# Weights from float64 to float32 on 16-bit halves, in a windowed attention with two MoE layers

## The chip, the cores and the metric

One core of one Trainium2 chip. The metric is the device time of one execution in microseconds (us); the number that counts is the median of several runs. The engines are PE (TensorE, matmuls), DVE (VectorE), ACT (ScalarE), POOL (GpSimd) and SP (SyncE, which issues the DMAs here).

## What is computed

Attention over 2 batches of 8 heads, 768 tokens and a head size of 64, where a token sees the first 4 tokens and a window of 128; then two dense layers on the 1536 tokens, each from 512 to 2048 and back to 512 columns. The weights come as float64.

```python
def _moe_ref(x, w_in, w_out):
    h = x @ w_in
    sp = np.where(h > 20.0, h, np.log1p(np.exp(np.minimum(h, 20.0))))
    g = h * np.tanh(sp)
    return (g @ w_out).astype(np.float32)

def _moe2_ref(x, w_in, w_out):
    h = x @ w_in
    g = h * np.clip(h + 3.0, 0.0, 6.0) / 6.0
    return (g @ w_out).astype(np.float32)

x = attention(q, k, v, n_sink, window)
x = _moe_ref(x, **moe)
return _moe2_ref(x, **moe2)
```

## The kernel before

The code counts the two dense layers as layer 0 and layer 1, and so does this text. The 2048 middle columns of a layer are cut into 16 chunks (`f`), the tokens into three blocks of 512. An `up` step multiplies tokens by the chunk's input weights (L728 to L730; `up2` for layer 1: L797 to L799), ACT and DVE apply the activation (L731 to L745; L801 to L815), and a `down` step multiplies by the output weights (L773; `down2`: L835). Every f32 operand goes to PE as two f16 parts, so each product is three matmuls.

The weights are float64 in HBM, and DVE makes float32 of them. `load_w` fetches one chunk of both matrices into the tile `raw` (two buffers; L166 and L170, on SP's queue). `gen_decode` reads it as 32-bit words, a low and a high word for each number, 1024 numbers in a partition, in three DVE operations on the tile `p`: L209 shifts and masks the high word, L210 puts in the top three bits of the low word, L211 puts in the sign and the top exponent bit. Then `p` is split into two f16 parts: for layer 0 on ACT (L218) and DVE (L220), for layer 1 in `split_pair` (ACT L245, L263; DVE L246, L256 to L259, L264), which works on pairs of chunks.

The three operations are right only for numbers whose exponent lies in a certain range, and a check sees to that. `exponents` takes the top 16 bits of each number on DVE (L184, into the tile `y`, one buffer, 16-bit elements) and lets ACT add them up (L188, which reads `y` as 512 whole words and leaves the sum in a column of `wchk`). For layer 1 that is done in `gen_decode`, just ahead of L209; for layer 0 its weights are fetched once more, late in the program (`gen_check`). A tail takes the largest of `wchk` (L971) and starts a general path if anything is out of range.

The decode of layer 0 runs beside the attention of the first two token blocks and layer 0's first steps. The `p` of layer 1 lies in a pool (`late["p"]`) that opens when attention is done, at about 262 us; from there its decode runs beside the last steps of layer 0 and the first of layer 1. The order of each engine's queue is not the order of the code: a scheduler of the framework places the instructions. An engine works its queue strictly in order.

Of the kernel before, what the change touches and what calls it, by code (L numbers as in the profile page):

```python
# [7 lines left out]
F32 = mybir.dt.float32  # L8
F16 = mybir.dt.float16
I32 = mybir.dt.int32  # L10
I16 = mybir.dt.int16
AF = mybir.ActivationFunctionType
ALU = mybir.AluOpType
# [16 lines left out]
def attention_moe_moe2(  # L30
# [13 lines left out]
    nc = tc.nc  # L44
# [4 lines left out]
    KF = DFF // 128  # L49
# [13 lines left out]
    dec_p = main.enter_context(tc.tile_pool(name="dec", bufs=1))  # L63
# [33 lines left out]
    wchk = keep.tile([128, 2 * KF], F32)  # L97
# [3 lines left out]
    def watch(ap):  # L101
        i = n_low[0]
        n_low[0] += 1
        sq = const.tile([128, 64], F32, tag="sq", name="sq")
        nc.vector.tensor_tensor_reduce(out=sq, in0=ap, in1=ap, scale=1.0, scalar=0.0, op0=ALU.mult, op1=ALU.max, accum_out=lows[:, i:i + 1])
# [50 lines left out]
    late = {}  # L156
# [16 lines left out]
    def load_w():  # L173
        if nload[0] >= len(wseq):
            return
        layer, f = wseq[nload[0]]
        nload[0] += 1
        raw_t[layer, f] = fetch_w(layer, f)

    def exponents(idx, t, pin=False):  # L180

        y = dec_p.tile([128, 1024], I16, tag="y", name="y")
        top = t.rearrange("p f t -> p (f t)").bitcast(I16).rearrange("p (f t) -> p f t", t=4)[:, :, 3]
        look = nc.vector.tensor_scalar(out=y, in0=top, scalar1=0x7800, scalar2=0x3800, op0=ALU.bitwise_and, op1=ALU.bitwise_xor)  # L184
        if pin:
            tc.keep_in_program_order(look)
        yy = y.bitcast(I32)
        nc.scalar.activation(out=yy, in_=yy, func=AF.Copy, accum_out=wchk[:, idx:idx + 1])  # L188

    def gen_check():  # L190


        ahead = []
        for f in range(KF + 2):
            if f > 1:
                exponents(f - 2, ahead.pop(0).rearrange("p a f t -> p (a f) t"), True)
            if f < KF:
                ahead.append(fetch_w(0, f))
            yield
            yield  # L200

    def gen_decode(idx):
        layer, f = wseq[idx]
        t = raw_t.pop((layer, f)).rearrange("p a f t -> p (a f) t")
        lo_w, hi_w = t[:, :, 0], t[:, :, 1]
        if layer == 1:
            exponents(idx, t)
        p = (late["p"] if layer == 1 else dec_p).tile([128, 1024], I32, tag="p", name="p")
        nc.vector.tensor_scalar(out=p, in0=hi_w, scalar1=3, scalar2=0x3FFFFFF8, op0=ALU.logical_shift_left, op1=ALU.bitwise_and)  # L209
        nc.vector.scalar_tensor_tensor(out=p, in0=lo_w, scalar=29, in1=p, op0=ALU.logical_shift_right, op1=ALU.bitwise_or)  # L210
        nc.vector.scalar_tensor_tensor(out=p, in0=hi_w, scalar=-0x40000000, in1=p, op0=ALU.bitwise_and, op1=ALU.bitwise_or)  # L211
        pf = p.bitcast(F32).rearrange("p (a f) -> p a f", a=2)
        load_w()
        if layer == 1:
            yield from split_pair(f, pf)
            return
        w = (w_a if f < KF // 2 else late["w_b"]).tile([128, 2, 2, 512], F16, tag="w", name="w")
        nc.scalar.activation(out=w[:, :, 0, :], in_=pf, func=AF.Copy, scale=2.0 ** SW)  # L218
        yield
        nc.vector.scalar_tensor_tensor(out=w[:, :, 1, :], in0=pf, scalar=2.0 ** SW, in1=w[:, :, 0, :], op0=ALU.mult, op1=ALU.subtract)  # L220
        wt[layer, 0, f] = w[:, 0]
        wt[layer, 1, f] = w[:, 1]
        if f == 0:
            watch(w[:, 0, 0, 0:64])
            watch(w[:, 1, 0, 0:64])
# [10 lines left out]
    def split_pair(f, pf):  # L236


        q = f % 2
        if q == 0:  # L240
            open_pair["w"] = slot()
            open_pair["p"] = []
        w = open_pair["w"]
        open_pair["p"].append(pf[:, 1])
        nc.scalar.activation(out=w[:, q, 0, :], in_=pf[:, 0], func=AF.Copy, scale=2.0 ** SW)  # L245
        nc.vector.scalar_tensor_tensor(out=w[:, q, 1, :], in0=pf[:, 0], scalar=2.0 ** SW, in1=w[:, q, 0, :], op0=ALU.mult, op1=ALU.subtract)  # L246
        wt[1, 0, f] = w[:, q]
        if f == 0:
            watch(w[:, 0, 0, 0:64])
        yield  # L250
        if q == 0:
            return
        p0, p1_ = open_pair.pop("p")
        b11, b12, b21, b22 = p0[:, 0:256], p0[:, 256:512], p1_[:, 0:256], p1_[:, 256:512]
        t = dec_p.tile([128, 4, 256], F32, tag="p", name="t")
        nc.vector.tensor_tensor(out=t[:, 0], in0=b12, in1=b11, op=ALU.subtract)  # L256
        nc.vector.tensor_tensor(out=t[:, 1], in0=b22, in1=t[:, 0], op=ALU.subtract)
        nc.vector.tensor_tensor(out=t[:, 2], in0=b22, in1=b12, op=ALU.subtract)
        nc.vector.tensor_tensor(out=t[:, 3], in0=t[:, 1], in1=b21, op=ALU.subtract)  # L259
        wx = [slot().rearrange("p a b (c n) -> p (a b) c n", c=2) for _ in range(2)]  # L260
        for dst, src in ((wx[0], t), (wx[1][:, 0], b11), (wx[1][:, 1:3], p1_.rearrange("p (a n) -> p a n", a=2))):
            hi = dst[..., 0, :]
            nc.scalar.activation(out=hi, in_=src, func=AF.Copy, scale=2.0 ** SW)  # L263
            nc.vector.scalar_tensor_tensor(out=dst[..., 1, :], in0=src, scalar=2.0 ** SW, in1=hi, op0=ALU.mult, op1=ALU.subtract)  # L264

        wt[1, 1, f // 2] = [wx[1][:, 0], wx[1][:, 1], wx[1][:, 2], wx[0][:, 3], wx[0][:, 0], wx[0][:, 1], wx[0][:, 2]]
        if f == 1:
            watch(wx[1][:, 0, 0, 0:64])
# [407 lines left out]
    def gen_weights():  # L676
        for idx in range(len(wseq)):
            for _ in gen_decode(idx):
                yield None
            yield ("dec", idx)  # L680
# [287 lines left out]
    nc.vector.tensor_scalar(out=bads[:, 1:2], in0=nsw[:, 1:2], scalar1=128.0, scalar2=None, op0=ALU.is_gt)  # L968
    nc.vector.scalar_tensor_tensor(out=bads[:, 1:2], in0=nsw[:, 1:2], scalar=1.0, in1=bads[:, 1:2], op0=ALU.is_lt, op1=ALU.max)

    nc.vector.tensor_reduce(out=bads[:, 2:3], in_=wchk, axis=AX.X, op=ALU.max)  # L971

    nc.vector.tensor_scalar(out=osum, in0=osum, scalar1=0.0, scalar2=0.0, op0=ALU.mult, op1=ALU.is_equal)
# [217 lines left out]
```

## Time and profile before

| what | us |
|---|---|
| median of 3 runs (lowest, highest) | 614.8 (614.75, 616.62) |
| the profiled execution: its own time | 618.45 |
| the profiled execution: span | 616.7 |
| busy in the span: PE, DVE, ACT, POOL | 581.9, 487.0, 393.2, 21.4 |

A busy share is a mean over stretches with different limits, so the stretches are to be read one by one: up to 100 us the first attention blocks, to 260 us the rest of attention beside layer 0, to 402 us the decode of layer 1, then layer 1 alone. A matmul's own duration is not its cost, since matmuls overlap; its cost is the step from one start to the next. The same holds in part on DVE and ACT: an instruction starts up to a tenth of a microsecond before the one ahead of it has ended.

### The profile page before, as it was taken

What the parts mean: (1) busy time and instruction counts of PE and PEld (TensorE: products, weight loads), DVE (VectorE), ACT (ScalarE), POOL (GpSimd) and SP (SyncE); (2) the same over time, 40 slices, a digit from 0 to 9 for tenths busy, and PEclk for the clock granted to TensorE, in tenths of its full rate; (3) what the DMA queues carried; (4) which work ended last, traced back from release to release, by engine and by line L of the source; (5) the groups of instructions that cost most, each with busy time, mean ns of one, the idle gap of its engine ahead of it and who ended that gap; (6) DMA issues with size and microseconds to landing.
All of it is one profiled execution on the core that took longest, in us unless ns stands there. A gap on an engine that the chain in (4) does not pass through costs nothing.

```text
span 616.7 us, 11401 instructions
## 1 busy us (share of the span) xinstructions
PE 581.9 (94%) x4424; PEld 394.9 (64%) x4424; DVE 487.0 (79%) x1132; ACT 393.2 (64%) x788; POOL 21.4 (3%) x36
## 2 busy tenths in 40 slices
PE   8999999789999999899999999899999999999991
PEld 4778664334544444444444468788888888888881
DVE  5889999689976345699999999996687888956652
ACT  5998686687788586578776873544355565534431
POOL 0130001400000000000000000000000000000000
PEclk9999999999999999999999999989999999999996
DMA  9884346997572213242335322400026667200001
GB/s 186 208 161 145 125 137 151 208 266 203 172 207 42 54 36 54 38 154 88 138 122 183 108 101 82 137 2 1 1 70 236 229 223 268 71 2 1 36 1 40
DMA packets 105847, 72.29 MB, mean 117 GB/s; under 512 B 73512, under 2 KB 98088, under 8 KB 105784
## 3 DMA queue, kind: packets, MB, share of 16 engines
q1 hardware_dynamic: 105784, 71.48, 41.7%
q8 instruction: 36, 0.59, 0.4%
q14 instruction: 27, 0.22, 0.1%
HBM read 60.43 MB, written 3.15 MB: 103 GB/s over the span
## 4 chain that ended last, share of the span: by engine, by line
PE 52%; DVE 30%; DMA 7%; ACT 4%; issue 3%; SPq 2%; POOL 0%; DVEq 0%; POOLq 0%
PE acc L835 17%; PE acc L773 5%; PE h L798 5%; PE h L799 5%; PE h L797 5%; DVE p L210 4%; DVE p L211 4%; DMA raw<-in_moe_w_out_dram 3%; DVE w L264 2%; PE h L728 2%; PE h L730 2%; PE h L729 2%; DVE p L209 2%; DVE g L745 2%; DVE e L740 2%
## 5 line engine op out<-in xcount | busy, mean ns | idle before, releaser
L773 PE MATMUL acc<-g,w 128*128 128x512 f16 x576 | 130.6, 379 | 4.6 <-DVE g L745 3.4
L835 PE MATMUL acc<-w,g 128*128 128x256 f16 x1008 | 115.8, 275 | 4.1 <-DVE ob L849 2.6
L835 PEld LDWEIGHTS <-g 128*128 128x128 f16 x1008 | 99.3, 99 | 17.2 <-issue 3.7
L798 PE MATMUL h<-xt,w 128*128 128x256 f16 x384 | 104.7, 273 | 0.0
L797 PE MATMUL h<-xt,w 128*128 128x256 f16 x384 | 104.7, 273 | 0.0
L799 PE MATMUL h<-xt,w 128*128 128x256 f16 x384 | 104.7, 273 | 0.0
L773 PEld LDWEIGHTS <-w 128*128 128x128 f16 x576 | 55.3, 98 | 71.4 <-issue 7.3
L728 PE MATMUL h<-xt,w 128*128 128x512 f16 x192 | 72.7, 379 | 4.5 <-DVE mins L549 3.0
L730 PE MATMUL h<-xt,w 128*128 128x512 f16 x192 | 72.8, 379 | 0.0
L729 PE MATMUL h<-xt,w 128*128 128x512 f16 x192 | 72.8, 379 | 0.0
L802 DVE SCALAR_TENSOR_TENSOR e<-e,h 128x512 f32<-128x512 f32 x48 | 32.8, 686 | 36.9 <-ACT e L801 36.8
L801 ACT ACTIVATE e<-h,bias 128x512 f32<-128x512 f32 x48 | 32.2, 676 | 38.5 <-PE h L799 38.5
L814 ACT ACTIVATE g<-sm 128x512 f16<-128x512 f32 x48 | 30.2, 629 | 31.3 <-DVE sm L809 30.9
L814 ACT ACTIVATE g<-e 128x256 f16<-128x256 f32 x96 | 29.4, 354 | 29.8 <-DVE e L802 29.2
L815 DVE SCALAR_TENSOR_TENSOR g<-sm,g 128x512 f16<-128x512 f32 x48 | 33.2, 691 | 10.1 <-ACT g L814 10.1
L731 ACT ACTIVATE e<-h 128x512 f32<-128x512 f32 x48 | 27.8, 586 | 20.4 <-PE h L730 20.3
L798 PEld LDWEIGHTS <-w 128*128 128x128 f16 x384 | 37.6, 98 | 4.6
L797 PEld LDWEIGHTS <-w 128*128 128x128 f16 x384 | 37.6, 98 | 4.5
L799 PEld LDWEIGHTS <-w 128*128 128x128 f16 x384 | 37.6, 98 | 4.4
L210 DVE SCALAR_TENSOR_TENSOR p<-raw,p 128x1024 int32<-128x1024 int32 x32 | 39.0, 1225 | 0.3
L211 DVE SCALAR_TENSOR_TENSOR p<-raw,p 128x1024 int32<-128x1024 int32 x32 | 39.0, 1221 | 0.1
L740 DVE SCALAR_TENSOR_TENSOR e<-e,h 128x512 f32<-128x512 f32 x48 | 30.9, 682 | 10.4 <-ACT e L738 10.4
(172 smaller groups left out, 953.5 us busy)
## 6 DMA issues: line engine op xcount, KB each, us to landing
raw<-in_moe_w_in_dram SPq DMA_DIRECT2D x48, 512.0 KB, 3.9
raw<-in_moe_w_out_dram SPq DMA_DIRECT2D x48, 512.0 KB, 4.6
out_dram<-ob SPq DMA_DIRECT2D x12, 256.0 KB, 2.1
first<-in_k_dram SPq DMA_DIRECT2D x8, 256.0 KB, 5.1
first<-in_q_dram SPq DMA_DIRECT2D x8, 256.0 KB, 5.2
first<-in_v_dram SPq DMA_DIRECT2D x8, 256.0 KB, 4.8
nk<-in_k_dram SPq DMA_DIRECT2D x5, 256.0 KB, 4.9
nv<-in_v_dram SPq DMA_DIRECT2D x5, 256.0 KB, 4.0
```

What stands on the lines that cost most here:

```text
L210: nc.vector.scalar_tensor_tensor(out=p, in0=lo_w, scalar=29, in1=p, op0=ALU.logical_shift_right, op1=ALU.bitwise_or)
L211: nc.vector.scalar_tensor_tensor(out=p, in0=hi_w, scalar=-0x40000000, in1=p, op0=ALU.bitwise_and, op1=ALU.bitwise_or)
L728: nc.tensor.matmul(o, wh, x[:, 0, c, :], start=c == 0, stop=False)
L729: nc.tensor.matmul(o, wh, x[:, 1, c, :], start=False, stop=False)
L730: nc.tensor.matmul(o, wl, x[:, 0, c, :], start=False, stop=c == KD - 1)
L740: nc.vector.scalar_tensor_tensor(out=e[:, i], in0=e[:, i], scalar=2.5, in1=hps[i], op0=ALU.subtract, op1=ALU.mult)
L773: nc.tensor.matmul(o, l_, r_, start=first and m == 0 and x == 0, stop=last and end and x == 2, skip_group_check=True)
L797: nc.tensor.matmul(o, wh, x[:, 0, c, :], start=c == 0, stop=False)
L798: nc.tensor.matmul(o, wh, x[:, 1, c, :], start=False, stop=False)
L799: nc.tensor.matmul(o, wl, x[:, 0, c, :], start=False, stop=c == KD - 1)
L814: nc.scalar.activation(out=g[:, 0, d_], in_=src, func=AF.Copy, scale=sc)
L835: nc.tensor.matmul(a[i // 2][:, i % 2], l_, r_, start=first and i % 2 == 0 and x == 0, stop=last and x == 2 and (i % 2 == 1 or i == NP - 1 ...
```

## The change

A weight is put together from two operations on 16-bit halves and one on whole words. In the changed kernel the tile `y` has whole words. L210 takes the top half of the high word, keeps its upper five bits, inverts them and writes them to the upper half of each word of `y`; L211 takes the top half of the low word, shifts its three top bits down and writes them to the lower half. L212 shifts the high word left by three and joins it with `y` by an exclusive or; that is `p`. For layer 1 the check reads the same `y`: L215 on ACT squares it in place as float32 (each element is plus or minus 2 with a small rest) and adds up 1024 squares. The call of `exponents`, its L184 and its L188, goes away for layer 1 and stays for layer 0. The tail has two more small operations on `wchk`.

```diff
--- before.py
+++ after.py
@@ -179,7 +179,7 @@
 
     def exponents(idx, t, pin=False):
 
-        y = dec_p.tile([128, 1024], I16, tag="y", name="y")
+        y = dec_p.tile([128, 1024], I32, tag="y", name="y").bitcast(I16)[:, 0:1024]
         top = t.rearrange("p f t -> p (f t)").bitcast(I16).rearrange("p (f t) -> p f t", t=4)[:, :, 3]
         look = nc.vector.tensor_scalar(out=y, in0=top, scalar1=0x7800, scalar2=0x3800, op0=ALU.bitwise_and, op1=ALU.bitwise_xor)
         if pin:
@@ -202,13 +202,17 @@
     def gen_decode(idx):
         layer, f = wseq[idx]
         t = raw_t.pop((layer, f)).rearrange("p a f t -> p (a f) t")
-        lo_w, hi_w = t[:, :, 0], t[:, :, 1]
+        halves = t.rearrange("p f t -> p (f t)").bitcast(I16).rearrange("p (f t) -> p f t", t=4)
+        y = dec_p.tile([128, 1024], I32, tag="y", name="y")
+        yh = y.bitcast(I16).rearrange("p (f t) -> p f t", t=2)
+        p = (late["p"] if layer == 1 else dec_p).tile([128, 1024], I32, tag="p", name="p")
+
+        nc.vector.tensor_scalar(out=yh[:, :, 1], in0=halves[:, :, 3], scalar1=-0x800, scalar2=-0x800, op0=ALU.bitwise_and, op1=ALU.bitwise_xor)
+        nc.vector.tensor_scalar(out=yh[:, :, 0], in0=halves[:, :, 1], scalar1=13, scalar2=7, op0=ALU.logical_shift_right, op1=ALU.bitwise_and)
+        nc.vector.scalar_tensor_tensor(out=p, in0=t[:, :, 1], scalar=3, in1=y, op0=ALU.logical_shift_left, op1=ALU.bitwise_xor)
         if layer == 1:
-            exponents(idx, t)
-        p = (late["p"] if layer == 1 else dec_p).tile([128, 1024], I32, tag="p", name="p")
-        nc.vector.tensor_scalar(out=p, in0=hi_w, scalar1=3, scalar2=0x3FFFFFF8, op0=ALU.logical_shift_left, op1=ALU.bitwise_and)
-        nc.vector.scalar_tensor_tensor(out=p, in0=lo_w, scalar=29, in1=p, op0=ALU.logical_shift_right, op1=ALU.bitwise_or)
-        nc.vector.scalar_tensor_tensor(out=p, in0=hi_w, scalar=-0x40000000, in1=p, op0=ALU.bitwise_and, op1=ALU.bitwise_or)
+            yf = y.bitcast(F32)
+            nc.scalar.activation(out=yf, in_=yf, func=AF.Square, accum_out=wchk[:, idx:idx + 1])
         pf = p.bitcast(F32).rearrange("p (a f) -> p a f", a=2)
         load_w()
         if layer == 1:
@@ -968,6 +972,8 @@
     nc.vector.tensor_scalar(out=bads[:, 1:2], in0=nsw[:, 1:2], scalar1=128.0, scalar2=None, op0=ALU.is_gt)
     nc.vector.scalar_tensor_tensor(out=bads[:, 1:2], in0=nsw[:, 1:2], scalar=1.0, in1=bads[:, 1:2], op0=ALU.is_lt, op1=ALU.max)
 
+    nc.vector.tensor_scalar(out=wchk[:, KF:], in0=wchk[:, KF:], scalar1=-4096.0, scalar2=1.0e6, op0=ALU.add, op1=ALU.min)
+    nc.vector.tensor_tensor(out=wchk[:, KF:], in0=wchk[:, KF:], in1=wchk[:, KF:], op=ALU.mult)
     nc.vector.tensor_reduce(out=bads[:, 2:3], in_=wchk, axis=AX.X, op=ALU.max)
 
     nc.vector.tensor_scalar(out=osum, in0=osum, scalar1=0.0, scalar2=0.0, op0=ALU.mult, op1=ALU.is_equal)
```

Three places in the engines' order. First DVE in the decode of chunks 4 and 5 of layer 1, before (rows of the parts of the pair ahead stand among them; `Activation_49`, `PE_49`, `DMAHW..` name the semaphores of ACT, PE and the DMAs):

```order
L184 TENSOR_SCALAR y<-raw 128x1024 [waits DMAHW7_49,DMAHW0_49]
L264 SCALAR_TENSOR_TENSOR w<-t,w 128x4x256 [waits Activation_49]
L264 SCALAR_TENSOR_TENSOR w<-p,w 128x256 [waits Activation_49]
L264 SCALAR_TENSOR_TENSOR w<-p,w 128x2x256 [waits Activation_49]
L209 TENSOR_SCALAR p<-raw 128x1024 [waits DVE_49] x2
L210 SCALAR_TENSOR_TENSOR p<-raw,p 128x1024 [waits DVE_49] x2
L211 SCALAR_TENSOR_TENSOR p<-raw,p 128x1024 [waits DVE_49]
L740 SCALAR_TENSOR_TENSOR e<-e,h 128x512 [waits Activation_49]
```

and in the changed kernel, whose line numbers are its own (L744 is L740 of before, L250 is L246, L260 is L256, L268 is L264):

```order
L212 SCALAR_TENSOR_TENSOR p<-raw,y 128x1024 [waits DVE_49]
L260 TENSOR_TENSOR t<-p 128x256 [waits DVE_49]
L210 TENSOR_SCALAR y<-raw 128x1024 [waits DMAHW7_49,DMAHW0_49,Activation_49]
L250 SCALAR_TENSOR_TENSOR w<-p,w 128x512 [waits Activation_49]
L211 TENSOR_SCALAR y<-raw 128x1024
L268 SCALAR_TENSOR_TENSOR w<-p,w 128x256 [waits PE_49,Activation_49]
L212 SCALAR_TENSOR_TENSOR p<-raw,y 128x1024 [waits DVE_49]
L744 SCALAR_TENSOR_TENSOR e<-e,h 128x512 [waits Activation_49]
L744 SCALAR_TENSOR_TENSOR e<-e,h 128x512
```

The decodes of the two chunks no longer run side by side: the first operation of the second one, L210, now waits for ACT, and between it and the L212 ahead stands one small operation, L260.

Second ACT, at the same place in the program, before:

```order
L188 ACTIVATE y,wchk<-y 128x512 [waits DVE_49,Activation_49]
L731 ACTIVATE e<-h 128x512 [waits PE_49]
L736 ACTIVATE e<-e,one 128x1024 [waits Activation_49]
L737 ACTIVATE e<-e,fifth 128x1024 [waits Activation_49]
L738 ACTIVATE e<-e 128x1024 [waits Activation_49]
L245 ACTIVATE w<-p 128x512 [waits DVE_49]
```

and in the changed kernel:

```order
L740 ACTIVATE e<-e,one 128x1024 [waits Activation_49]
L215 ACTIVATE y,wchk<-y 128x1024 [waits DVE_49]
L249 ACTIVATE w<-p 128x512
L741 ACTIVATE e<-e,fifth 128x1024 [waits Activation_49]
L267 ACTIVATE w<-p 128x256
L742 ACTIVATE e<-e 128x1024 [waits Activation_49]
L215 ACTIVATE y,wchk<-y 128x1024 [waits DVE_49]
```

The check now stands behind L212 of its own chunk, among the steps of the activation (L740 to L742), and ahead of the first split of `p` (L249).

Third SP's queue at about 107 us, where the loads of attention (`nk`, `nv`, `nq`, the transposes `kt`, `qt`) and of weights (`raw`) share it, before:

```order
L592 DMA vsn<-in_v_dram 64x1x64 x4
L473 DMA nk<-in_k_dram 128x8x64
L473 DMA nv<-in_v_dram 128x8x64
L166 DMA raw<-in_moe_w_in_dram 128x4x256
L496 DMA_TRANSPOSE kt_1479<-k_1476 128x8x128
L473 DMA nk<-in_k_dram 128x8x64
```

and in the changed kernel:

```order
L596 DMA vsn<-in_v_dram 64x1x64 x4
L477 DMA nv<-in_v_dram 128x8x64
L500 DMA_TRANSPOSE kt_1486<-k_1483 128x8x128
L526 DMA_TRANSPOSE qt<-q_1533 128x8x128
L477 DMA nq<-in_q_dram 128x8x64
L477 DMA nk<-in_k_dram 128x8x64
L477 DMA nv<-in_v_dram 128x8x64
L166 DMA raw<-in_moe_w_in_dram 128x4x256
```

There the weights' load `raw` stood between two loads of attention, and it now stands behind a transpose of `q` and three loads.

## Rows read from the trace of the kernel before

**Rows 1.** Engines by stretch: stretch; busy us and instructions per engine; clock; DMA share; GB/s.

```profile
20.00:100.00 80.00, 76.97 (x675) 55.58 (x676) 74.69 (x199) 63.57 (x158) 8.72 (x14) 1.00 0.56 154
...
100.00:180.00 80.00, 73.32 (x445) 34.02 (x443) 69.24 (x107) 63.13 (x102) 10.91 (x12) 1.00 0.83 197
...
260.00:402.00 142.00, 134.89 (x803) 76.49 (x802) 138.81 (x235) 98.26 (x158) 0.00 (x0) 1.00 0.36 121
```

**Rows 2.** Groups, 260 to 402 us: out<-in form xcount | busy us, mean ns | idle before, releaser.

```profile
L773 PE MATMUL acc<-g,w 128*128 128x512 f16 x240 | 54.2, 379 | 3.0 <-DVE g L745 2.9
...
L729 PE MATMUL h<-xt,w 128*128 128x512 f16 x70 | 26.5, 379 | 0.0
...
L798 PE MATMUL h<-xt,w 128*128 128x256 f16 x80 | 21.8, 273 | 0.0
...
L835 PE MATMUL acc<-w,g 128*128 128x256 f16 x88 | 10.7, 275 | 4.1 <-DVE ob L849 2.6 <-DVE g L815 0.8 <-ACT w L245 0.7
...
L619 PE MATMUL o<-vs,atg 128*128 128x256 f16 x1 | 0.3, 283 | 1.7 <-DMA atg<-ag 1.7
```

**Rows 3.** Chain that ended last, whole run: start us, us, what; PE at full rate.

```profile
203.77 5.18 PE acc L773 x24
...
417.89 4.58 PE acc L835 x42
```

**Rows 4.** Groups, 260 to 402 us: the decode of layer 2 weights on DVE.

```profile
L209 DVE TENSOR_SCALAR p<-raw 128x1024 int32<-128x1024 int32 x16 | 10.9, 692 | 0.0
...
L210 DVE SCALAR_TENSOR_TENSOR p<-raw,p 128x1024 int32<-128x1024 int32 x16 | 19.4, 1224 | 0.0
...
L211 DVE SCALAR_TENSOR_TENSOR p<-raw,p 128x1024 int32<-128x1024 int32 x16 | 19.5, 1224 | 0.0
...
L184 DVE TENSOR_SCALAR y<-raw 128x1024 int16<-128x1024 int16 x14 | 9.7, 694 | 0.5 <-DMA raw<-in_moe_w_out_dram 0.5
```

**Rows 5.** Chain that ended last, 260 to 402 us: shares by line.

```profile
by line: DVE p L210 12.8%; DVE p L211 12.2%; DVE w L264 10.3%; issue 6.8%; DVE w L246 6.6%; DVE p L209 6.3%; DVE e L740 5.4%; DVE y L184 5.1%; DVE g L745 5.0%; DVE g L815 3.8%; DVE xt L887 3.4%; DMA raw<-in_moe_w_out_dram 3.2%; DVE e L802 2
```

**Rows 6.** Groups, 20 to 100 us: a decode step of layer 1 weights.

```profile
L210 DVE SCALAR_TENSOR_TENSOR p<-raw,p 128x1024 int32<-128x1024 int32 x8 | 9.8, 1230 | 0.1
```

**Rows 7.** Chain that ended last, 20 to 100 us: first and last of five decode pieces.

```profile
33.02 0.69 DVE p L209
...
64.26 1.23 DVE p L210
```

**Rows 8.** Chain that ended last, 100 to 180 us: shares by line.

```profile
by line: DMA raw<-in_moe_w_out_dram 14.7%; PE acc L773 13.1%; DMA qt<-q 12.1%; issue 9.2%; DVE p L211 5.9%; DVE p L210 4.6%; DMA nk<-in_k_dram 4.3%; ACT g L744 4.0%; DVE g L745 3.1%; SPq L592 2.8%; SPq L166 2.3%; DVE q L520 2.2%; PE h L729 
```

**Rows 9.** Groups, 100 to 180 us: a decode step of layer 1 weights.

```profile
L210 DVE SCALAR_TENSOR_TENSOR p<-raw,p 128x1024 int32<-128x1024 int32 x8 | 9.8, 1224 | 0.2
```

**Rows 10.** Groups, 260 to 402 us: ACT forms, and DVE work beside the decode.

```profile
L738 ACT ACTIVATE e<-e 128x1024 f32<-128x1024 f32 x9 | 9.4, 1047 | 0.1
...
L188 ACT ACTIVATE y<-y 128x512 int32<-128x512 int32 x14 | 8.7, 621 | 3.1 <-DVE y L184 3.0
...
L188 ACT ACTIVATION_READ_ACCUMULATOR y<-y 128x1 f32 x14 | 2.6, 187 | 0.0
...
L256 DVE TENSOR_TENSOR t<-p 128x256 f32<-128x256 f32 x8 | 3.4, 422 | 0.0
...
L740 DVE SCALAR_TENSOR_TENSOR e<-e,h 128x512 f32<-128x512 f32 x18 | 11.6, 683 | 0.0
...
L264 DVE SCALAR_TENSOR_TENSOR w<-t,w 128x1024 f16<-128x1024 f32 x8 | 9.8, 1229 | 1.6 <-ACT w L263 1.6
```

**Rows 11.** Timeline, 184 to 186 us: one check from DVE to ACT (start us, us, operation).

```profile
184.00 0.69 DVE L184 TENSOR_SCALAR y<-raw 128x1024 int16<-128x1024 int16 x1 [3.18 <-DMA raw<-in_moe_w_out_dram]
...
184.73 0.63 ACT L188 ACTIVATE y<-y 128x512 int32<-128x512 int32 x1 [0.61 <-DVE y L184]
...
185.26 0.19 ACT L188 ACTIVATION_READ_ACCUMULATOR y<-y 128x1 f32 x1
```

**Rows 12.** Engines by stretch, 400 to 420 us: the granted clock.

```profile
400.00:420.00 20.00, 18.35 (x153) 15.80 (x153) 18.99 (x58) 10.91 (x25) 0.00 (x0) 0.91 0.01 1
```

## The prediction, made before the changed kernel ran

> **What bounds the kernel now.** I first read the busy time of the engines by stretch, since the mean over the span hides three different limits. From 20 to 100 us DVE is busy 74.7 of 80 us, but PE 77.0 as well and ACT 63.6: attention, where short work passes from engine to engine. From 100 to 180 us DVE is busy 69.2 of 80. From 260 to 402 us DVE is busy 138.8 of 142 us, 98%, and is the limit [rows 1]. After 402 us matmuls follow each other at their full rate [rows 3], and no decode is left.
>
> So what can be won lies ahead of 402 us, and PE sets the floor. In 260 to 402 us the groups of PE show 240 + 3 x 70 wide matmuls (512 columns; L728 to L730 have 69 or 70 each) and 3 x 80 + 88 narrow ones (256 columns; L797 to L799 have 80 each) [rows 2]. At full rate 24 wide ones take 5.18 us, 0.216 each, and 42 narrow ones 4.58 us, 0.109 each [rows 3]. That is 449 x 0.216 + 328 x 0.109 = 132.7 us of 142: PE loses 9.3 us, and 1.7 of these are a wait for a DMA of attention, not for DVE [rows 2]. No more than about 7.6 us can come back there, however fast the decode gets.
>
> **The cost of a decode.** Before, it takes 0.69 + 1.22 + 1.22 = 3.14 us of DVE, and for layer 1 another 0.69 for the check's first half: 3.83 [rows 4]. The new whole-word operation reads two tiles of 1024 words as L210 does: 1.22. The two operations on halves have one input, as L184 and L209 have. L184 reads 16-bit elements with a step of four at 0.69, L209 32-bit words with a step of two at 0.69 [rows 4]; what no row shows is a result whose 16-bit elements lie two apart. It is bounded by 0.69, the price of L184, and by 1.22, the price of one element after the other; I take 0.69, since L184 differs only in where its results lie. The sum is 2 x 0.69 + 1.22 = 2.61: 0.53 us less in layer 0, 1.22 us less in layer 1.
>
> [...]
>
> **Layer 0, 16 decodes.** Eight run from 20 to 100 us [rows 6] and save 8 x 0.53 = 4.2 us. Of their 25.1 us only five pieces, 4.9 us together, stand on the chain that ended last [rows 7], a fifth; I count a fifth, 0.8 us. Eight more run from 100 to 180 us [rows 9]. There L210 and L211 hold 10.5% of the chain, 8.4 of their 19.6 us [rows 8, 9], about 40%; I count 1.7 us. The rest of that chain is DMA (raw 14.7%, a transpose of q 12.1%). SP's order also moves the weights' loads behind the loads of attention; either may gain by it, and I count nothing, with one load either way in the range.
>
> **Layer 1, 16 decodes.** L209, L210, L211 and L184 take 10.9 + 19.4 + 19.5 + 9.7 = 59.5 us there [rows 4], and hold 36% of the chain [rows 5], 51 of 142 us. After: 16 x 1.22, and 30 of the 32 operations on halves (chunk 0 has both done early, as L184 has now), 20.8, together 40.4. DVE is rid of 19.1 us.
>
> Against it stands a new wait. `y` has one buffer, so L210 of a chunk waits until ACT has squared the `y` of the chunk ahead, and all of DVE's queue behind it waits too, the activations that PE needs among it. A square of 1024 elements costs as L738, 1.05 us, where L188 cost 0.62 [rows 10]; an ACT sum takes 0.09 us beyond its operation and starts 0.04 us after DVE has ended [rows 11]. So L210 may start 1.05 + 0.09 + 2 x 0.04 = 1.22 us after L212 has ended, if ACT is free. In DVE's order three chunks (3, 5, 13) have only L260 in between, 0.42 us [rows 10], and wait 0.8 us each: 2.4 us. The other twelve have at least 1.1 us of DVE work in between (L261 to L263 at 0.42 each, or two L744 at 0.68), and wait next to nothing. ACT is busy 98.3 of 142 us [rows 1], mostly in pieces of about 1 us, so some squares start late. I put all waits at 5 us; the bounds are 2.4, and 19 if each of the fifteen stands behind one more piece of 1.1 us. ACT itself gets 16 x 0.43 = 7 us more, and has 44 free.
>
> DVE then has 19.1 - 5 = 14 us less to do, more than PE's 7.6 us, and PE becomes the limit. I count 6.0 of the 7.6, as a part of PE's waits is a handing over from ACT and DVE that a free DVE keeps. The tail's two small operations stand in the order long before the end, beside layer 1's steps, where PE is the limit: nothing.
>
> **The sum.** 0.8 + 1.7 + 6.0 = 8.5 us. The profiled execution took 618.45 us and would take 609.9; it is 3.65 us above the median, so I subtract the gain from the median: 614.8 - 8.5 = **606.3 us**.
>
> **Rivals.**
> [...]
> - *The square holds DVE.* If each of the fifteen waits averages 1.3 us, the 19.1 us are gone and only layer 0 gains: 612.3. For it: ACT's queue has 1.1 us pieces right ahead of most squares. Against it: twelve of fifteen are covered.
> - *The order costs what layer 0 gains.* From 100 to 180 us loads of raw hold 14.7% of the chain, 11.8 us [rows 8]. If they come so much later, behind attention's loads, that this grows by half, 5.9 us go: 612.2. For it: raw now stands three loads further back in SP's queue at 107 us. Against it: those loads are themselves on the chain.
> - *Slower: results on half words run one by one.* Then an operation on halves costs 1.22 us and a decode 3.67. Layer 0 loses 0.53 a decode, by the same shares 0.8 + 1.7 = 2.5 us. Layer 1 needs 16 x 1.22 + 30 x 1.22 = 56.1 in place of 59.5 us, and the 5 us of waits make a loss of 1.6. In all 618.9. It decides from 0.96 us an operation, where layer 0 stops gaining. For it: no row has such a result. Against it: L184, with 16-bit results.
>
> **How the numbers follow.** The forecast (602 to 610) has 0.62; more than that 0.10; the square 0.08; the order 0.08; half words 0.12. A measurement of this kernel tells 0.3% from no change, 1.8 us: faster is below 613.0, slower above 616.6. Faster takes the forecast, the gain beyond it, most of the square's case and half of the order's: 0.80. Slower is the half words: 0.12. The rest, 0.08, is the same. The range runs from 600.4, the end of the larger gain, to 616.0, which takes in the square and the order and leaves out the half words.
>
> **What would show it.** Right: L210 and L211 at about 0.69 us and L212 at 1.22; from 260 us on, DVE waiting for ACT's L215 at a few places for about 0.8 us; the same matmuls done some 6 us sooner, with L773's wait for L749 near nothing; layer 1 alone at 0.109 us a matmul as before. Wrong: an operation on halves near 1.2 us; waits for L215 of over 1 us on most chunks; a gain that lies ahead of 260 us for the most part; or PE still waiting for DVE with DVE not busy.

## The result, and the profile after

The changed kernel takes **607.08 us** (median of 4 runs, 606.50 to 607.38), the kernel before 615.71 beside it (4 runs, 614.75 to 616.73): the ratio is 0.9838, with a 95% interval of 0.9818 to 0.9858. It is faster by 8.6 us. The forecast was 606.3.

The profiled execution took 607.09 us with a span of 605.3; that of before took 618.45 with a span of 616.7. The two spans differ by 11.4 us, 2.7 more than the medians, since the profiled execution of before took longer than each of the four runs. What follows compares these two traces.

The first view is the engines by stretch in the changed kernel (stretch, then busy us and instructions of PE, PEld, DVE, ACT and POOL, then granted clock, DMA share, GB/s).

```profile
20.00:100.00 80.00, 76.55 (x671) 55.48 (x672) 73.74 (x206) 65.06 (x160) 11.28 (x14) 1.00 0.57 157
100.00:180.00 80.00, 75.27 (x465) 35.15 (x464) 63.79 (x110) 63.65 (x104) 8.13 (x12) 1.00 0.81 204
...
260.00:402.00 142.00, 139.50 (x845) 82.34 (x844) 132.64 (x252) 109.65 (x175) 0.00 (x0) 1.00 0.36 121
400.00:420.00 20.00, 20.00 (x186) 17.92 (x184) 13.88 (x42) 8.04 (x18) 0.00 (x0) 1.00 0.00 1
```

Beside [rows 1, 12]: from 260 to 402 us PE is busy 139.5 of 142 us where it was 134.9, and DVE has 9 us free where it had 3. ACT carries 11 us more. At 400 to 420 us the granted clock is 1.00 where it was 0.91. From 20 to 100 us little has changed.

The groups of the changed kernel, 260 to 402 us, on DVE, for the decode of layer 1:

```profile
L212 DVE SCALAR_TENSOR_TENSOR p<-raw,y 128x1024 int32<-128x1024 int32 x15 | 18.3, 1221 | 0.1
...
L210 DVE TENSOR_SCALAR y<-raw 128x1024 int16<-128x1024 int16 x15 | 11.3, 753 | 2.9 <-ACT y L215 2.6
L211 DVE TENSOR_SCALAR y<-raw 128x1024 int16<-128x1024 int16 x15 | 11.2, 747 | 0.0
```

An operation on halves takes 0.75 us, near L184's 0.69 and far from 1.22. In this window the decode takes 18.3 + 11.3 + 11.2 = 40.8 us where it took 59.5 ([rows 4], whose heading counts the layers from one). But the changed kernel is 3 us earlier here, and the window leaves out one operation of the first chunk, which starts ahead of it:

```profile
258.75 1.23 DVE L212 SCALAR_TENSOR_TENSOR p<-raw,y 128x1024 int32<-128x1024 int32 x1
```

With it the decode takes 42.0 us, so DVE is rid of 17.5 us. The new wait for the square is there and small. The waits of the changed kernel, 258 to 392 us (engine and line, what it waited for: us in total, times, longest us), show both sides of it:

```profile
ACT y L215 <- DVE p L212: 7.5, 8, 1.7
DVE y L210 <- ACT y L215: 2.6, 4, 0.8
PE acc L777 <- DVE g L749: 2.0, 2, 1.1
...
PE acc L839 <- DVE ob L853: 0.4, 1, 0.4
```

DVE waits for ACT in four places, 2.6 us in all and 0.8 at most; ACT waits for DVE longer than that. In the decode of chunks 4 and 5 DVE's rows run as they stand in its queue, from 293.44 to 300.51 us: L210 starts at 295.87 after 0.76 us of waiting, and L250, L211, L268, L212 and L744 behind it. PE waited 2.9 us for L745 ahead of L773, and 4.1 us ahead of L835, 2.6 of them for L849 [rows 2]. Now it is 2.0 and 0.4, so most of what came back lies ahead of L835.

Where did the time come from? Two marks that both kernels have: the single matmul L619 (L623 after), where attention's last part ends, and the start of the last block of layer 1's matmuls, L835 (L839 after). The timeline and the chain that ended last, before:

```profile
259.89 0.28 PE L619 MATMUL o<-vs,atg 128*128 128x256 f16 x1 [1.73 <-DMA atg<-ag]
```

```profile
401.65 11.00 PE acc L835 x84
...
594.74 8.86 PE acc L835 x81
```

and in the changed kernel:

```profile
256.89 0.28 PE L623 MATMUL o<-vs,atg 128*128 128x256 f16 x1 [1.72 <-DMA atg<-ag]
```

```profile
388.00 4.75 PE acc L839 x42
...
584.66 8.86 PE acc L839 x81
```

3.0 us are won ahead of the first mark and 10.08 - 3.0 = 7.1 between the two. The last 1.3 of the 11.4 us lie behind the last small operation on DVE (8.4 us to the end of the span before, 7.1 after; the runs below show 6.1 to 8.6 there, with either tail), so they cannot be put down to the change.

Of the 7.1 us, some 1.7 are the clock. At full rate, a granted clock of 1.00, 84 of these matmuls take 2 x 4.58 = 9.16 us [rows 3]; before, they took 11.00 behind PE's wait of 2.6 us, 1.84 more. The block of 42 of the changed kernel behind its wait of 0.4 takes 4.75, 0.17 more. The other 5.4 us are waits. Between the marks both kernels run the same 2551 matmuls; counted from the traces by the step from one matmul to the next, waits cost PE 8.4 us there before and 3.0 after. Here is the clock around the end of the wait of before, 400 to 405 us:

```profile
400.00:405.00 5.00, 3.35 (x18) 2.43 (x18) 5.00 (x17) 2.41 (x6) 0.00 (x0) 0.70 0.00 0
```

The stretch up to the first mark is mixed: the step on DVE that the timeline shows at 83.36 us before (L740) comes at 85.04, 1.7 us later; the one at 107.28 comes at 108.87, 1.6 later; and the one at 125.65 comes at 121.92, 3.7 sooner.

### The profile page after: what moved, and what is told of

It is laid out like the page before. It is cut to its first block, busy times and chain, and to the rows that moved or that the text cites. A ratio compares the mean times of both kernels' runs of the same rounds, so it can differ in the third digit from the quotient of the medians.

```text
span 605.3 us, 11399 instructions
## 1 busy us (share of the span) xinstructions
PE 579.6 (96%) x4424; PEld 394.8 (65%) x4424; DVE 464.3 (77%) x1118; ACT 397.8 (66%) x788; POOL 21.2 (4%) x36
## 4 chain that ended last, share of the span: by engine, by line
PE 55%; DVE 27%; ACT 7%; DMA 5%; issue 3%; SPq 1%; POOL 0%; DVEq 0%; ACTq 0%
PE acc L839 17%; PE acc L777 7%; PE h L801 6%; PE h L802 6%; PE h L803 6%; DVE p L212 3%; DVE e L744 3%; PE h L732 3%; PE h L734 3%; PE h L733 3%; DVE g L749 2%; DMA raw<-in_moe_w_out_dram 2%; DVE y L211 2%; DVE w L268 2%; DVE y L210 2%
## 5 line engine op out<-in xcount | busy, mean ns | idle before, releaser
L839 PE MATMUL acc<-w,g 128*128 128x256 f16 x1008 | 113.8, 273 | 0.4 <-DVE ob L853 0.4
L839 PEld LDWEIGHTS <-g 128*128 128x128 f16 x1008 | 98.6, 98 | 12.1 <-issue 0.7
L777 PEld LDWEIGHTS <-w 128*128 128x128 f16 x576 | 55.2, 98 | 69.2 <-issue 4.4
L819 DVE SCALAR_TENSOR_TENSOR g<-sm,g 128x512 f16<-128x512 f32 x48 | 32.9, 686 | 11.4 <-ACT g L818 11.4
L801 PEld LDWEIGHTS <-w 128*128 128x128 f16 x384 | 37.6, 98 | 4.6
L802 PEld LDWEIGHTS <-w 128*128 128x128 f16 x384 | 37.6, 98 | 4.5
L803 PEld LDWEIGHTS <-w 128*128 128x128 f16 x384 | 37.6, 98 | 4.3
L212 DVE SCALAR_TENSOR_TENSOR p<-raw,y 128x1024 int32<-128x1024 int32 x32 | 39.5, 1234 | 0.4
L744 DVE SCALAR_TENSOR_TENSOR e<-e,h 128x512 f32<-128x512 f32 x48 | 30.7, 682 | 11.5 <-ACT e L742 11.2
L734 PEld LDWEIGHTS <-w 128*128 128x128 f16 x192 | 18.8, 98 | 22.6
```

What stands on the lines that cost most here:

```text
L212: nc.vector.scalar_tensor_tensor(out=p, in0=t[:, :, 1], scalar=3, in1=y, op0=ALU.logical_shift_left, op1=ALU.bitwise_xor)
L734: nc.tensor.matmul(o, wl, x[:, 0, c, :], start=False, stop=c == KD - 1)
L744: nc.vector.scalar_tensor_tensor(out=e[:, i], in0=e[:, i], scalar=2.5, in1=hps[i], op0=ALU.subtract, op1=ALU.mult)
L777: nc.tensor.matmul(o, l_, r_, start=first and m == 0 and x == 0, stop=last and end and x == 2, skip_group_check=True)
L801: nc.tensor.matmul(o, wh, x[:, 0, c, :], start=c == 0, stop=False)
L802: nc.tensor.matmul(o, wh, x[:, 1, c, :], start=False, stop=False)
```

## The experiments

The theory was A: layer 1's stretch gives some 7 us, because DVE is rid of enough work that PE sets the pace; layer 0 adds a little because its decode is shorter. The rivals: the gain lies in layer 0; it comes from the queues' order, not from decode time; the square's wait still holds PE; any DVE time taken off layer 1 would have paid. This table gives, for each run, the two marks and the stretch between them (from the timeline and the chain), and the ratio to the kernel before on the same chip.

| kernel | L619 | last block | between | ratio, 95% interval |
|---|---|---|---|---|
| before | 259.89 | 594.74 | 334.85 | |
| the change | 256.89 | 584.66 | 327.77 | 0.9838 (0.9818 to 0.9858) |
| new decode in layer 1 alone | 259.67 | 587.52 | 327.85 | 0.9847 (0.9823 to 0.9871) |
| new decode in layer 0 alone | 257.10 | 592.25 | 335.15 | 0.9950 (0.9929 to 0.9971) |
| change, second `y` | 257.52 | 586.72 | 329.20 | 0.9845 (0.9822 to 0.9867) |
| before, layer 1 not checked | 258.38 | 592.55 | 334.17 | 0.9947 (0.9929 to 0.9965) |
| change, L211 twice in layer 1 | 256.94 | 592.11 | 335.17 | 0.9934 (0.9913 to 0.9954) |
| change, L211 twice in layer 0 | 257.99 | 585.76 | 327.77 | 0.9837 (0.9814 to 0.9859) |
| change, both halves twice in layer 0 | 260.31 | 588.23 | 327.92 | 0.9894 (0.9859 to 0.9928) |
| before, L209 twice in layer 0 | 258.91 | 593.69 | 334.78 | 0.9955 (0.9930 to 0.9979) |

The marks are those of one execution of each kernel, and they move without a cause that the rows of the queues show. Up to the first mark SP's queue and PE's are the same, row for row, and ACT's and DVE's all but a few rows, in before, layer 1 alone and layer 1 not checked; these three reach it at 259.89, 259.67 and 258.38. The same holds among the change, layer 0 alone, second `y`, L211 twice in layer 1 and the kernel of the last experiment below; these five reach it at 256.89, 257.10, 257.52, 256.94 and 258.10. So the first mark moves by 1.2 to 1.5 us by itself, and the means, 259.3 and 257.3, lie 2.0 apart. The stretch between the marks is steadier: 327.77 to 327.92 in the four kernels of the table that have the new decode in layer 1, one `y` and nothing twice there.

### Which layer

```diff
+        if layer == 1:
+            halves = t.rearrange("p f t -> p (f t)").bitcast(I16).rearrange("p (f t) -> p f t", t=4)
...
+        else:
+            lo_w, hi_w = t[:, :, 0], t[:, :, 1]
+            if layer == 1:
+                exponents(idx, t)
...
```

That is the first kernel; in the second it is `if layer == 0:`, and the tail's two operations go, since its check is the old one.

> The new decode and the check on its tile for layer 1 alone; layer 0 as before, so the queues up to 260 us stand as before. Theory A (in the stretch from 260 us DVE was the limit, and every us taken off it comes back until PE is): nothing changes ahead of 260 us, some 7 us come back behind it, ratio near 0.988, DVE no longer full there. Rival B (layer 1 only gains because layer 0 is ready earlier): ratio within 0.003 of 1.

> The new decode for layer 0 alone; layer 1 with its three operations and its separate check as before. Theory A: the 3 us that the profile of the change shows ahead of 260 us, and nothing more, ratio near 0.995; the stretch from 260 us stays full on DVE. Rival B (both layers are needed): under 1 us, ratio over 0.998.

Layer 1 alone: 608.73 us (5 runs; before 617.64 on that chip). Layer 0 alone: 614.65 (7 runs). In the marks the two parts stand apart and add up. With the new decode in layer 1 alone the first mark stays (-0.2) and the stretch behind it is shorter by 7.0; with that in layer 0 alone the first mark comes 2.8 sooner and the stretch stays (+0.3). Layer 1 gives 7; layer 0 gives 2.8 in this pair of traces and 2.0 between the means above. The medians add up less well: 8.9 + 3.0 = 11.9 us here, where the whole change gained 8.6 beside its own runs of before. Layer 1 alone (0.9847) and the whole change (0.9838) cannot be told apart by them, so what layer 0 adds to layer 1 rests on the traces.

### Is the square's wait worth removing

```diff
-        y = dec_p.tile([128, 1024], I32, tag="y", name="y")
+        y = (late["y"] if layer == 1 and f % 2 else dec_p).tile([128, 1024], I32, tag="y", name="y")
```

> The changed kernel with a second tile y for the odd chunks of layer 1, so that a decode need not wait for the square of the one ahead. Theory A: the waits for ACT on DVE, 2.6 us in the profile of the change, go to near nothing, and the time moves by under 1 us against the change (606 to 607 us), since PE is the limit. Rival D (that wait still holds PE): 2 to 3 us less than the change, near 604.

608.38 us (5 runs). The waits of this kernel, 258 to 410 us, on DVE and then on PE:

```profile
DVE e L807 <- ACT e L806: 5.8, 4, 3.2
DVE g L820 <- ACT g L819: 3.0, 6, 0.5
DVE y L210 <- DMA raw<-in_moe_w_out_dram: 2.4, 1, 2.4
```

```profile
PE acc L778 <- DVE g L750: 3.9, 4, 1.4
```

No wait for the square is left, and PE waits longer for the activation on DVE (3.9 against 2.0): the stretch is 1.4 us longer than in the change. Taking the 2.6 us away won nothing, and the rival's 2 to 3 us did not come. The second `y` also gave the queues another order, so what the wait costs in the order of the change is not shown by itself.

### What a microsecond of DVE is worth in layer 1

Two kernels stand between before and the change in DVE's work. The first leaves layer 1's check out of the kernel before:

```diff
-        if layer == 1:
-            exponents(idx, t)
...
+    nc.vector.memset(wchk, 0.0)
```

> The kernel before, without the check of layer 1's exponents (its operation on DVE and its sum on ACT are left out), the three operations of the decode as they were. DVE loses 16 x 0.69 = 11 us of the 19 that the change takes off it. Theory A: 4 to 6 us come back, ratio near 0.992, as PE could regain 7.6 at most. Rival C (the conversion's own time is what counts, the check was hidden): under 1 us.

The second puts work back into the change:

```diff
         nc.vector.tensor_scalar(out=yh[:, :, 0], in0=halves[:, :, 1], scalar1=13, scalar2=7, op0=ALU.logical_shift_right, op1=ALU.bitwise_and)
+        if layer == 1:
+            nc.vector.tensor_scalar(out=yh[:, :, 0], in0=halves[:, :, 1], scalar1=13, scalar2=7, op0=ALU.logical_shift_right, op1=ALU.bitwise_and)
```

> The change, with L211 issued twice in every decode of layer 1: 16 x 0.75 = 12 us more for DVE from 260 to 402 us, which leaves it some 5 us less work there than before the change. Theory A, PE is the limit there with room to spare: 607 to 609. Theory B, DVE's backlog at the end of that stretch decides (the run without layer 1's check, rid of 11 us of DVE, gained only 2.2 at the end): most of layer 1's 7.1 us go, 612 to 614, with a wait of PE for L853 of over 2 us near 395 us and a granted clock under 1 behind it.

614.46 us (9 runs) and 613.62 (5 runs). The first has 9.7 us of DVE work less than before in this stretch [rows 4] and gains 0.7 there. By the medians it is 3.2 us faster, but the rest of what its trace has won lies ahead of the first mark, 1.5 us, where its order is that of before, and behind the last small operation, 2.3 us, so it cannot be put down to the check. The second has these groups from 260 to 402 us:

```profile
L214 DVE SCALAR_TENSOR_TENSOR p<-raw,y 128x1024 int32<-128x1024 int32 x16 | 19.7, 1230 | 0.3
L213 DVE TENSOR_SCALAR y<-raw 128x1024 int16<-128x1024 int16 x15 | 11.4, 762 | 0.2
L210 DVE TENSOR_SCALAR y<-raw 128x1024 int16<-128x1024 int16 x15 | 11.4, 757 | 2.1 <-ACT y L217 1.9
L211 DVE TENSOR_SCALAR y<-raw 128x1024 int16<-128x1024 int16 x15 | 11.3, 755 | 0.0
```

They are 53.8 us, so DVE is rid of 5.7, and nothing is gained between the marks (+0.3). The change, rid of 17.5, gains 7.1. So the gain is not in proportion to DVE's time; where between 9.7 and 17.5 us it sets in, and how sharply, no run shows. The row of PE's longest wait, the stretch around it and the block behind it, without the check:

```profile
PE acc L833 <- DVE ob L847: 4.0, 1, 4.0
```

```profile
380.00:400.00 20.00, 16.03 (x125) 13.19 (x123) 19.47 (x51) 10.24 (x22) 0.00 (x0) 0.83 0.28 97
...
395.00:400.00 5.00, 5.00 (x30) 3.72 (x28) 4.50 (x17) 2.49 (x6) 0.00 (x0) 0.60 0.00 0
```

```profile
393.81 7.27 PE acc L833 x42
```

and with L211 twice in layer 1:

```profile
PE acc L841 <- DVE ob L855: 3.8, 1, 3.8
```

```profile
380.00:400.00 20.00, 16.18 (x126) 13.15 (x124) 20.00 (x54) 11.31 (x26) 0.00 (x0) 0.83 0.31 106
...
395.00:400.00 5.00, 5.00 (x25) 3.47 (x24) 5.00 (x17) 1.86 (x5) 0.00 (x0) 0.50 0.00 0
```

```profile
394.78 7.27 PE acc L841 x42
```

and in the change:

```profile
380.00:400.00 20.00, 19.56 (x180) 17.32 (x178) 17.70 (x52) 10.71 (x24) 0.00 (x0) 1.00 0.10 37
```

In the two kernels PE runs into a DVE that is still full (19.5 and 20.0 of 20 us), waits for `ob` for 4 us, and then runs the block of 42 at a lowered clock: 7.27 us in either, 4.58 at full rate. That is 4 + 2.7 = 6.7 us at one place. In the change DVE is at 17.7 of these 20 us and the wait is 0.4. Counted from the traces, PE's matmuls from the first mark on take, in us:

| kernel | the first 703 | the next 180, with the longest wait |
|---|---|---|
| before | 128.5 | 24.1 |
| before, layer 1 not checked | 125.6 | 26.3 |
| change, L211 twice in layer 1 | 126.8 | 26.2 |
| the change | 125.3 | 20.3 |

So DVE time taken off does pay up to here, by 1.8 to 3.3 us. The two kernels between lose it again at this one place, where they wait longer than before; the change gains another 3.8 there. The expectation of 4 to 6 us for the check alone failed, as decode time was priced by the microsecond. In these four kernels, what the stretch is worth hangs on whether DVE has caught up at that place.

### Layer 0: decode time, or the order of the queues

Three kernels make a decode of layer 0 dearer than it is before the change (3.14 us) or in the change (2.73): L211 twice (3.5 us), both half-word operations twice (4.2), and, in the kernel before, L209 twice (3.8).

```diff
         nc.vector.tensor_scalar(out=yh[:, :, 0], in0=halves[:, :, 1], scalar1=13, scalar2=7, op0=ALU.logical_shift_right, op1=ALU.bitwise_and)
+        if layer == 0:
+            nc.vector.tensor_scalar(out=yh[:, :, 0], in0=halves[:, :, 1], scalar1=13, scalar2=7, op0=ALU.logical_shift_right, op1=ALU.bitwise_and)
+            nc.vector.tensor_scalar(out=yh[:, :, 1], in0=halves[:, :, 3], scalar1=-0x800, scalar2=-0x800, op0=ALU.bitwise_and, op1=ALU.bitwise_xor)
```

This is the second kernel; the first has no last line.

```diff
         nc.vector.tensor_scalar(out=p, in0=hi_w, scalar1=3, scalar2=0x3FFFFFF8, op0=ALU.logical_shift_left, op1=ALU.bitwise_and)
+        if layer == 0:
+            nc.vector.tensor_scalar(out=p, in0=hi_w, scalar1=3, scalar2=0x3FFFFFF8, op0=ALU.logical_shift_left, op1=ALU.bitwise_and)
```

> The change, with L211 issued twice in every decode of layer 0: a decode of layer 0 takes 0.75 + 0.75 + 0.75 + 1.22 = 3.47 us of DVE, 0.33 more than before the change and 0.75 more than with it; layer 1 is as in the change. Theory A, the gain ahead of 260 us is decode time: it turns into a loss of about 1 us against the kernel before, so the same instruction at 260 us stands near +1 in place of -3.0, and the run takes 607.1 + 4 = 611. Theory B, it comes from the order of the loads in SP's queue: at 260 us it stays near -3, if the order stays, and the run takes 607 to 608. If the order changes again and the place at 260 us goes by more than either, order weighs more than decode time, whatever its sign.

> The change, with both half-word operations issued twice in every decode of layer 0: 0.75 x 4 + 1.22 = 4.2 us, 1.1 more than before the change, 17 us more of DVE ahead of 180 us than before it. SP's queue comes out in yet another order. Theory A, decode time of layer 0 counts by its share of the chain (a fifth to two fifths): 4 to 6 us later at 260 us than the change, 611 to 613. Theory B, only the order of the queues counts there: within about 2 us of the change, 605 to 609, on either side.

> The kernel before, with L209 issued twice in every decode of layer 0: 0.69 more a decode, 3.83 us, 11 us more of DVE ahead of 180 us. Theory A (decode time): 2.5 to 4 us later at 260 us than the kernel before, 618 to 620 on a chip that gives 616 for it. Theory B (order): anything within 3 us of before on either side, a gain too, with a constant shift from about 200 us on.

607.56 us (4 runs), 610.22 (4 runs) and 614.60 (10 runs, before 617.22 on that chip): the first and the third as the order would have it, the second between its two expectations. Engines by stretch, 20 to 180 us, in the kernel before, in the change, and in these three in this order:

```profile
20.00:180.00 160.00, 150.29 (x1118) 89.59 (x1119) 143.93 (x305) 126.70 (x260) 19.63 (x26) 1.00 0.70 175
```

```profile
20.00:180.00 160.00, 151.82 (x1135) 90.63 (x1136) 137.53 (x313) 128.71 (x264) 19.41 (x26) 1.00 0.69 180
```

```profile
20.00:180.00 160.00, 151.65 (x1121) 90.24 (x1120) 148.29 (x326) 127.06 (x261) 20.52 (x26) 1.00 0.71 180
```

```profile
20.00:180.00 160.00, 151.41 (x1121) 90.82 (x1121) 153.18 (x337) 126.42 (x258) 26.48 (x26) 1.00 0.69 174
```

```profile
20.00:180.00 160.00, 152.85 (x1121) 90.98 (x1121) 145.19 (x315) 125.10 (x256) 23.54 (x26) 1.00 0.66 163
```

DVE does between 137.5 and 153.2 us of work here. By count PE has done 1135 matmuls in the change, 1121 in each of the other three edits and 1118 before. With L211 twice the decode is dearer than before, and the first mark still comes at 257.99, sooner than in any of the three kernels with the order of before. With L209 twice in the kernel before it comes at 258.91, within what that order shows without the edit (258.38 to 259.89), and not 2.5 to 4 us later. So the shorter decode alone does not explain layer 0's gain. By its median that last kernel is even 2.6 us faster than the one with less work; beside the trace of before, its trace is 1.0 us sooner at the first mark and 2.0 shorter behind the last small operation, so where its gain comes from is open. Dearer decodes within the changed form do cost something: some 12 and 24 us more of DVE put the mark at 257.99 and 260.31, 0.7 and 3.0 us behind the mean of the change's order; the first is within what the mark moves by itself, the second loses the whole gain. Each edit gives SP's queue another order of loads, and PE, ACT and DVE another order too. The order is thus the rival that is left for the rest of layer 0's gain. What sets the two groups apart is not chance: at the step that before has at 125.65 us the five kernels with the change's order are at 121.7 to 122.0, the three with that of before at 125.4 to 126.4. But the groups differ in decode time as well, and no run moved the order alone, so it is not shown by itself.

### The half-word operation by itself

```diff
+        nc.vector.tensor_scalar(out=d1[0], in0=s4, scalar1=-0x800, scalar2=-0x800, op0=ALU.bitwise_and, op1=ALU.bitwise_xor)
+        nc.vector.tensor_scalar(out=d2[1][:, :, 1], in0=s4, scalar1=-0x800, scalar2=-0x800, op0=ALU.bitwise_and, op1=ALU.bitwise_xor)
+        nc.vector.tensor_scalar(out=d2[2][:, :, 0], in0=s4, scalar1=13, scalar2=7, op0=ALU.logical_shift_right, op1=ALU.bitwise_and)
+        nc.vector.tensor_scalar(out=d2[3][:, :, 1], in0=s1, scalar1=-0x800, scalar2=-0x800, op0=ALU.bitwise_and, op1=ALU.bitwise_xor)
+        nc.vector.tensor_scalar(out=d1[4], in0=s1, scalar1=-0x800, scalar2=-0x800, op0=ALU.bitwise_and, op1=ALU.bitwise_xor)
+        nc.vector.tensor_scalar(out=d32[5], in0=src.rearrange("p (f t) -> p f t", t=2)[:, :, 1], scalar1=3, scalar2=0x3FFFFFF8, op0=ALU.logical_shift_left, op1=ALU.bitwise_and)
```

> The change, with twelve operations on 1024 columns added behind the last step, where DVE, PE and ACT have nothing else to do; each form twice. Theory A, the result's step of two costs the 0.06 us: reading 16-bit halves with a step of four and writing them densely takes 0.69, writing them two apart takes 0.75, for the mask and for the shift alike. Theory B, it is the neighbourhood (reads of raw while DMAs fill it, ACT beside DVE): all of them take 0.69 here. Theory C, the step of four in the read costs it together with the result's step: dense halves in and two apart out takes 0.69. Dense in and dense out is a base, under 0.69 if a step costs anything at all.

Here `s4` is every fourth 16-bit element of a tile and `s1` are adjacent ones; `d1` is dense and `d2` has the two halves of each word apart. One run, 610.46 us with the added work. The timeline of that kernel behind the last step, DVE (start us, us, operation):

```profile
591.99 0.68 DVE L1002 TENSOR_SCALAR mb<-src 128x1024 int16<-128x1024 int16 x1
592.58 0.75 DVE L1003 TENSOR_SCALAR mb<-src 128x1024 int16<-128x1024 int16 x1
593.22 0.74 DVE L1004 TENSOR_SCALAR mb<-src 128x1024 int16<-128x1024 int16 x1
593.85 0.74 DVE L1005 TENSOR_SCALAR mb<-src 128x1024 int16<-128x1024 int16 x1
594.47 0.41 DVE L1006 TENSOR_SCALAR mb<-src 128x1024 int16<-128x1024 int16 x1
594.80 0.68 DVE L1007 TENSOR_SCALAR mb<-src 128x1024 int32<-128x1024 int32 x1
```

The second round of each gives the same to 0.01 us. The result's step of two costs the 0.06 us (L1003 against L1002), for the mask and the shift alike (L1004), and a dense read does not take it back (L1005). In layer 1 of the change, beside loads and ACT, the two operations take 0.75 as well, so neighbours add nothing that shows.

## Why the prediction was right, and where not

**The decode.** Two operations on halves at 0.69 were the forecast; they take 0.75, at the lower bound's side, so a decode is 2.73 us in place of 2.61. DVE is rid of 17.5 us in layer 1 where 19.1 were counted; 30 operations at 0.06 us more are the difference. The rival with half words one by one (1.22) is out by L1003 to L1005: a result with its elements two apart costs 0.06 us for 1024 elements. The 1.22 is the time of the old L210, with two inputs; that it is the price of one element after the other no run shows.

**The square.** 5 us of waits were put down; they are 2.6, next to the lower bound of 2.4, the longest at the 0.8 us worked out. The rival that the square holds DVE falls by this row; that the second `y` takes the waits away and gains nothing agrees.

**Layer 1.** The mechanism held: DVE was the limit, and with less to do it let PE go on. 6.0 us were counted of PE's loss of 7.6, and no change of the clock. The 7.6 was too low: the 1.7 us wait taken off it ends at 259.89, ahead of the stretch, while some 0.8 us of attention's last matmuls lie in it; that leaves 8.5, near the 8.4 us of waits in the trace. The stretch gave 7.1, of which 1.7 is the clock that no longer falls; without it 5.4. No run shows the larger gain that ends the range at 600.4; what came beyond the count is the clock's 1.7: it was 0.70 from 400 to 405 us before, around the end of the wait for L849, and 1.00 from 388.00 to 392.75 us in the change, behind the wait for L853. One sign of being right failed: L773's wait for L749 was to be near nothing and is 2.0 us, and most of the gain came ahead of L835. And the prediction missed how near the edge this lies: it took PE's loss as something that DVE time buys back, and the runs that took off 9.7 and 5.7 us kept 0.7 and nothing.

**Layer 0.** The weak step. The sum of 0.8 + 1.7 = 2.5 us is near the 3.0 of the trace and the 2.0 between the means, but by luck: it priced decode time by the decode's share of the chain, a fifth to two fifths, and 12 and 24 us more of decode moved the mark by only 0.7 and 3.0 us, 6 and 12%. At that price the 6.5 us saved would give 0.4 to 0.8. The split was wrong too: at 83 us the change was 1.7 us behind, and all of the gain came after 100 us. The prediction counted nothing for the moved loads, and gave the order a rival that only loses; what the order gave by itself stays open.

**The tail.** Its two operations cost nothing that shows.

**The sum.** 8.5 us were forecast, 8.6 came between the medians. In the two traces the parts are 3.0 + 5.4 + 1.7 = 10.1, and the profiled execution of before is 2.7 us above its median in these runs; with 2.0 for layer 0 they are 9.1. The terms agree to a microsecond or two, not better, and the closeness of 8.5 to 8.6 is luck: layer 0 was right for the wrong reason, PE's waits gave 0.6 less than counted, and the clock's 1.7 made up for it.

## What to carry to other kernels

Time taken off a feeding engine can be lost again further on. Here two edits put PE 1.8 and 2.9 us ahead and lost it in one wait, with the lower clock behind it, at a place where the feeding engine had not caught up; a larger edit kept its lead and gained there too. So look for the place where the other engine next runs dry, and price the edit there, not by busy time alone. A share of the chain that ended last says what stood there in one order of the queues; if the edit lets a scheduler write another order, test the term with an edit that makes the same work dearer, and first see how far the mark moves between kernels of the same order. A wait that looks new and certain may cost little: take it away in an experiment before spending memory on it.

## What the runs showed of the hardware

- On 1024 columns of 16 bits in SBUF, a one-input operation on DVE takes 0.41 us dense to dense, 0.68 with a step of four in the read, and 0.74 to 0.75 with a step of two in the result, the read stepped or dense (L1002 to L1006).
- PE's granted clock was 0.70 in the 5 us around the end of a wait of 2.6 us for DVE, and 0.60 and 0.50 from 395 to 400 us, behind waits of 4.0 and 3.8 that ended at 393.81 and 394.78. Behind the 1.7 us for L619's DMA it was 1.00, from 259.9 to 265 us. The block behind the waits of about 4 us took 2.7 us more than at full rate (7.27 against 4.58, where the granted clock was 1.00).
